# A fused decode block on one core: w2 in 27 and 29 rows, fewer VectorE instructions, the output projection in two column groups, gate and up in quadrants of 992 columns

## The chip, the cores and the metric

The kernel runs on one core of one Trainium2 chip. The metric is device time in microseconds (us), measured over several runs of one launch. Beside it stands one execution taken by the hardware profiler, which gives a page of views and a trace that can be asked for more. The engines are named as in the profile: PE is TensorE's matmul (PEld its weight load), DVE is VectorE, ACT is ScalarE, POOL is GpSimd, SP is SyncE, which issues nearly all DMAs here.

## What is computed

One decode step of a transformer block for 4 sequences: attention over the last 2048 positions of a cache, then a gated MLP, each behind a layer norm and with a residual. All data are bf16. Cut to what matters:

```python
B, Sq, D = 4, 1, 1024            # Hq, Hkv, Sk, Dh = 32, 4, 8192, 128; F = 3584; W = 2048

def A(x):                        # attention
    q = (x @ wq).reshape(B, Sq, Hq, Dh).transpose(0, 2, 1, 3)
    k = repeat(k_cache[:, :, Sk - W:, :], 8, axis=1)
    v = repeat(v_cache[:, :, Sk - W:, :], 8, axis=1)
    p = softmax(einsum("bhqd,bhkd->bhqk", q, k) * Dh ** -0.5)
    o = einsum("bhqk,bhkd->bhqd", p, v)
    return o.transpose(0, 2, 1, 3).reshape(B, Sq, Hq * Dh) @ wo

def M(x):                        # MLP
    return (silu(x @ w1) * (x @ w3)) @ w2

h = x + A(layernorm(x))
h2 = h + M(layernorm(h))
```

Each weight and each used row of the cache is read once: wq, wo 8 MB each, k and v 8 MB each, w1, w3 and w2 7 MB each. With 4 rows of activations there is little arithmetic for each byte.

## The kernel before

**The ring.** All large inputs go through `stream`, five slots of 32 KB a partition (4 MB). `ring` (line 107) lists what takes a slot, in order: k of sequences 0 and 1, k of 2 and 3, the first half of wq, two slots for the transposed keys kT (written by engines, no DMA), the second half of wq, v in two slots, wo in two, w1, w3 in two each, and w2 in two: 16 rows, then 8, 2 and 2 rows as three transfers (`W2B`, line 108). "Row" means one of the 28 rows of w2 that each of the 128 partitions holds. `fill` (line 119) issues on SP's queue, at line 133, all transfers for which a slot is free; `done` (line 140) is called where a part has been used and calls `fill`. The instructions of each engine stand in the order of the program; SP's issues wait in its queue for the semaphores of the engines that last used the slot. A transfer's landing is counted by 16 increments of a semaphore, one from each DMA engine.

**Stages, in the order of TensorE's instructions.**

- Constants (lines 147 to 190) are made on DVE and POOL; x is loaded on ACT's queue (line 149). `layernorm_T` (line 192) works on the transposed rows: squares, a matmul with ones for the sums, mean, variance, Sqrt on ACT (line 208), reciprocal, and the product into `n_T`.
- k: 256 transposes on TensorE (line 241), eight to a PSUM bank; the 32 banks are copied into kT by DVE and ACT in turn (lines 243, 245).
- q: wq in four column groups of 32 output rows each (line 259), copied to SBUF by DVE and ACT, half each (269, 270), transposed, and spread into `Qm` by four DVE copies (279).
- Attention: for each of the four sequences `scores` (four column groups, line 294), `row_max` (308 to 317), `softmax` (323 to 334, four Exp on ACT), `transpose_p` (a DVE transpose, 346), `output` (tot 355, o_ps 369, od 378 and om 386 on DVE). The loop at line 390 staggers them: TensorE starts the scores of one sequence while the one before is at its maximum.
- Output projection: on_ps (409), on_sb, oX, oP on DVE (417 to 422), then 128 matmuls of 256 columns, four column groups, `y_ps` (434); h1 adds x (444), then the second layer norm (LN2).
- MLP: `up_projection` (450) for w1 ("gate") and w3 ("up"), each in four column groups with 2 x 448 of the 896 columns of a group (458); Exp on ACT (472), add 1, reciprocal and product on DVE (473 to 476), hg (480), its transpose hg_T (482), and 112 matmuls with w2 into `y2_ps` (491, "y_ps" in the profile), residual (501) and two stores (503, 504).

The core of the ring:

```python
while len(taken) < len(ring):
    n = len(taken) - NSLOT
    if n >= 0 and not all((name, i) in used for name, i, _, _ in ring[n]):
        break
    parts = ring[len(taken)]
    slot = stream.tile([P, SLOT], BF16, tag="slot", name="s_" + parts[0][0])
```

Of the kernel before, what the change touches and what calls it, by code (L numbers as in the profile page):

```python
# [10 lines left out]
P = 128  # L11
# [12 lines left out]
def kernel(  # L24
# [30 lines left out]
    FC = F // P  # L55
# [5 lines left out]
    FQ = F // C  # L61
    FH = FQ // 2
    assert B == C and Hkv == C and B * Hq == P and Dh == P and REP * Hkv == R
    assert D == KC * P and F == FC * P and W == NK * P and NQ == Hq * Dh
# [14 lines left out]
    w2_v = B_w2.rearrange("(p fc) n -> p fc n", fc=FC)  # L79
# [21 lines left out]
    wo_ = pair([("wo", g, [1, T * D], wo_v[:, g : g + 1, :]) for g in range(Hkv)])  # L101
# [6 lines left out]
    W2B = [16, 8, 2, 2]  # L108
# [5 lines left out]
    ring += [w2_[:1], w2_[1:]]  # L114
# [4 lines left out]
    def fill():  # L119
# [7 lines that stand above are left out]
            o = 0  # L127
            for name, i, shape, src in parts:
                dst = slot[:, o : o + int(np.prod(shape))]
                o += int(np.prod(shape))  # L130
                view = dst.rearrange("p (a b) -> p a b", a=shape[0])
                if src is not None:
                    nc.sync.dma_start(out=dst if name in ("k", "v") else view, in_=src)  # L133
                views[(name, i)] = view
            taken.append(slot)
# [4 lines left out]
    def done(name, i):  # L140
# [7 lines left out]
    nc.vector.memset(x_nat[:], 0.0)  # L148
    nc.scalar.dma_start(out=x_nat[::S, :], in_=x_flat.rearrange("b (c n) -> c b n", c=C))
    fill()  # L150

    ident = const.tile([P, P], BF16)
    make_identity(nc, ident[:])
    ones_f = const.tile([P, P], FP32)
    nc.vector.memset(ones_f[:], 1.0)
    eps_t = const.tile([P, 1], FP32)
    nc.vector.memset(eps_t[:], eps)

    t32 = const.tile([P, R], FP32)
    nc.vector.tensor_reduce(  # L160
        out=t32[:], in_=ident[:].rearrange("p (q h) -> p h q", q=C), axis=AX.X, op=ALU.add
    )
    ident_f = const.tile([P, P], FP32)
    nc.gpsimd.tensor_copy(out=ident_f[:], in_=ident[:])
    same = const.tile([P, C, R], FP32)
    for q in range(C):
        nc.gpsimd.tensor_copy(out=same[:, q], in_=t32[:])
# [4 lines left out]
    nc.vector.tensor_scalar(  # L172
# [3 lines left out]
    nc.vector.tensor_reduce(  # L176
        out=jmask[:, :, 0], in_=ident[:].rearrange("p (j h) -> p j h", j=JM), axis=AX.X, op=ALU.add
    )
    nscale = const.tile([P, Hkv], FP32)
    nc.vector.memset(nscale[:], -qscale)  # L180
# [3 lines left out]
    for l in range(2):  # L184
        nc.gpsimd.tensor_copy(
# [6 lines left out]
    def layernorm_T(h_T, tag):  # L192

        both = act.tile([P, 2, KC, B], FP32, tag=tag + "_both")
        nc.vector.tensor_copy(out=both[:, 0], in_=h_T[:, :, ::S])
        nc.vector.tensor_tensor(out=both[:, 1], in0=both[:, 0], in1=both[:, 0], op=ALU.mult)  # L196
        sums_ps = ps.tile([P, 2, KC, B], FP32, tag="kt3")
        nc.tensor.matmul(sums_ps[:], lhsT=ones_f[:], rhs=both[:], start=True, stop=True)  # L198
        sums = act.tile([P, 2, B], FP32, tag=tag + "_sums")
        nc.vector.tensor_reduce(  # L200
            out=sums[:], in_=sums_ps[:].rearrange("p t k b -> p t b k"), axis=AX.X, op=ALU.add
        )
        mean = act.tile([P, 2, B], FP32, tag=tag + "_mean")
        nc.vector.tensor_single_scalar(out=mean[:], in_=sums[:], scalar=1.0 / D, op=ALU.mult)
        rstd = act.tile([P, 1, B], FP32, tag=tag + "_rstd")
        nc.vector.tensor_tensor(out=rstd[:, 0], in0=mean[:, 0], in1=mean[:, 0], op=ALU.mult)
# [7 lines left out]
        hc = act.tile([P, KC, B], FP32, tag=tag + "_hc")  # L214
# [14 lines left out]
    x_T = act.tile([P, KC, R], BF16)  # L229
# [5 lines left out]
    for b in range(B):  # L235
        k = get("k", b)
        kT = get("kT", b)
        for jb in range(JR // JB):
# [3 lines left out]
            if n_step % 2 == 0:  # L242
# [7 lines left out]
    q_ps = [ps.tile([P, REP // 2, Dh], FP32, tag=f"sc{hf}", name=f"q_ps{hf}") for hf in range(2)]  # L250
    HALF = REP // 2
    for i in range(KC // 4):
        w = get("wq", i)
        for kk in range(4):
            kc = 4 * i + kk
            for hf in range(2):
                for c in range(C):
                    o = (2 * c + hf) * HALF * Dh
                    nc.tensor.matmul(  # L259
                        q_ps[hf][R * c : R * c + R],  # L260
# [8 lines left out]
    nc.vector.tensor_copy(out=q_sb[:, :HALF], in_=q_ps[0][:])  # L269
    nc.scalar.copy(out=q_sb[:, HALF:], in_=q_ps[1][:])  # L270
# [7 lines left out]
    for b in range(B):  # L278
        nc.vector.tensor_copy(  # L279
            out=Qm[:, b].rearrange("p (g y) -> p g y", y=QW)[:, :, :REP],  # L280
            in_=qT_ps[:, :, :, S * b].rearrange("p r g -> p g r"),
        )


    sc_ps = [ps.tile([P, W // C], FP32, tag=f"sc{b}", name=f"sc_ps{b}") for b in range(B)]
    rs = act.tile([P, B, Hkv], FP32)
    om = act.tile([P, B, Dh], FP32)
    stage = {}

    def scores(b, gs):  # L290
        v = get("kT", b).rearrange("p j (q i g) -> p g q j i", q=C, g=Hkv)
        for g in gs:
            for q in range(C):
                nc.tensor.matmul(  # L294
                    sc_ps[b][R * q : R * q + R],
# [9 lines left out]
    def row_max(b):  # L305

        rmax = act.tile([P, 1], FP32, tag="rmax", bufs=2)
        nc.vector.reduce_max(out=rmax[:], in_=sc_ps[b][:], axis=AX.X)  # L308
        mx_ps = ps.tile([P, P], FP32, tag="kt3")
        nc.tensor.matmul(  # L310
            mx_ps[:1, :], lhsT=rmax[:], rhs=ident_f[:], start=True, stop=True
        )
        qmax = act.tile([1, C, R], FP32, tag="qmax", bufs=2)
        nc.vector.tensor_reduce(
            out=qmax[:, 0], in_=mx_ps[:1, :].rearrange("o (q h) -> o h q", q=C), axis=AX.X, op=ALU.max
        )
        nc.vector.tensor_copy(out=qmax[:, 1:], in_=qmax[:, 0:1].to_broadcast([1, C - 1, R]))
        stage[("qmax", b)] = qmax

    def softmax(b):  # L320

        nm_ps = ps.tile([P, Hkv], FP32, tag="kt3")
        nc.tensor.matmul(  # L323
            nm_ps[:],
            lhsT=stage.pop(("qmax", b))[:].rearrange("o q h -> o (q h)"),
            rhs=nscale[:1, :],
            start=True,
            stop=True,
        )
        bias = act.tile([P, Hkv], FP32, tag="bias", bufs=2)  # L330
        nc.vector.tensor_tensor(out=bias[:], in0=nm_ps[:], in1=negm[:], op=ALU.add)  # L331
        P4 = ktpool.tile([P, JR, L5, Hkv], BF16, tag="P4")
        for g in range(Hkv):
            nc.scalar.activation(  # L334
                out=P4[:, :, :, g],
                in_=sc_ps[b][:].rearrange("p (j i) -> p j i", i=L5),
                func=ACT.Exp,
                bias=bias[:, g : g + 1],
# [3 lines left out]
        stage[("P4", b)] = P4  # L342

# [9 lines left out]
    def output(b):  # L353
        tot_ps = ps.tile([P, Hkv], FP32, tag="kt3")
        nc.tensor.matmul(  # L355
            tot_ps[:],
            lhsT=same[:].rearrange("p q h -> p (q h)"),
            rhs=rs[:, b, :],
            start=True,
            stop=True,  # L360
        )
        rinv = act.tile([P, 1], FP32, tag="rinv", bufs=2)
        nc.vector.tensor_reduce(out=rinv[:], in_=tot_ps[:], axis=AX.X, op=ALU.add)
        nc.vector.reciprocal(out=rinv[:], in_=rinv[:])
# [3 lines left out]
        for i in range(JR // JM):  # L368
# [12 lines left out]
            scalar=rinv[:, 0:1],  # L381
# [4 lines left out]
        nc.vector.tensor_reduce(  # L386
            out=om[:, b], in_=od[:].rearrange("p j d -> p d j"), axis=AX.X, op=ALU.add
        )

    for b in range(B + 1):  # L390
        if b < B:
            scores(b, (0, 1))
        if b > 0:
            row_max(b - 1)
        if b < B:
            scores(b, (2, 3))
        if b > 0:
            softmax(b - 1)
        if b > 1:
            transpose_p(b - 2)  # L400
        if b > 2:
            output(b - 3)
    transpose_p(B - 1)
    output(B - 2)
    output(B - 1)
# [11 lines left out]
    nc.vector.tensor_copy(out=on_sb[:], in_=on_ps[:].rearrange("p l d -> p (l d)"))  # L417
    oX = act.tile([P, T, R], BF16)
# [3 lines left out]
    nc.vector.tensor_copy(  # L422
# [5 lines left out]
    y_ps = ps.tile([P, DQ], FP32, tag="kt0")  # L428
    for g in range(Hkv):
        w = get("wo", g)  # L430
        for t in range(T):
            for c in range(C):
                o = t * D + c * DQ
                nc.tensor.matmul(  # L434
                    y_ps[R * c : R * c + R, :],
                    lhsT=oP[:, g, t, :],
                    rhs=w[:, 0, o : o + DQ],
                    start=(g == 0 and t == 0),
                    stop=(g == Hkv - 1 and t == T - 1),
                    tile_position=(0, R * c),  # L440
                )
        done("wo", g)
    h1 = act.tile([P, DQ], FP32)
    nc.vector.tensor_tensor(out=h1[:], in0=y_ps[:], in1=x_nat[:], op=ALU.add)
    h_T = act.tile([P, KC, R], FP32)
    transpose_quads(h_T[:], h1[:], KC)
    hn_T = layernorm_T(h_T[:], "ln2")


    def up_projection(name, out_ps):  # L450
        for i in range(KC // 4):
            w = get(name, i)
            for kk in range(4):
                kc = 4 * i + kk
                for hf in range(2):
                    for c in range(C):
                        o = c * FQ + hf * FH
                        nc.tensor.matmul(  # L458
                            out_ps[hf][R * c : R * c + R],
# [8 lines left out]
    gu_ps = [ps.tile([P, FH], FP32, tag=f"sc{i}", name=f"gu_ps{i}") for i in range(4)]  # L468
    up_projection("w1", gu_ps[:2])
    eg = act.tile([P, 2, FH], FP32)  # L470
    for hf in range(2):
        nc.scalar.activation(out=eg[:, hf], in_=gu_ps[hf][:], func=ACT.Exp, scale=-1.0)
    nc.vector.tensor_scalar_add(out=eg[:], in0=eg[:], scalar1=1.0)
    nc.vector.reciprocal(out=eg[:], in_=eg[:])
    for hf in range(2):
        nc.vector.tensor_tensor(out=eg[:, hf], in0=gu_ps[hf][:], in1=eg[:, hf], op=ALU.mult)
    up_projection("w3", gu_ps[2:])
    hg = act.tile([P, 2, FH], BF16)
    for hf in range(2):
        nc.vector.tensor_tensor(out=hg[:, hf], in0=gu_ps[2 + hf][:], in1=eg[:, hf], op=ALU.mult)  # L480
    hg_T = act.tile([P, FC, R], BF16)
    transpose_quads(hg_T[:], hg[:].rearrange("p a f -> p (a f)"), FC)


    y2_ps = ps.tile([P, DQ], FP32, tag="kt1")
    fc = 0
    for i, n in enumerate(W2B):
        w = get("w2", i)
        for ff in range(n):
            for c in range(C):  # L490
                nc.tensor.matmul(  # L491
# [43 lines left out]
```

## Time and profile before

| | us |
|---|---|
| median of 3 runs | 140.03 (139.76, 140.03, 140.13) |
| the profiled execution's own time | 140.13 |
| its span in the profile | 138.3 |
| busy PE / PEld | 80.2 / 47.5 |
| busy DVE / ACT / POOL | 52.9 / 42.7 / 4.2 |
| DMA: 55.72 MB, mean | 403 GB/s |
| granted TensorE clock, mean | 0.781 |

The span is the time from the first instruction to the last; the device time has 1.8 us more around it. The page divides the span into 40 slices of some 3.5 us and shows the busy share of each engine in tenths, the granted clock of TensorE, and the share of time in which the 16 DMA engines moved data. The chain of waits is followed back from the last instruction: at each step to what released it. The timeline gives for each run of like instructions its start, its length, and, in brackets, the idle time of the engine before it and what ended that.

### The profile page before, as it was taken

How to read it: one execution, taken by the hardware profiler on the slowest of the kernel's cores; microseconds unless marked ns; L12 is line 12 of the kernel's file. 1: busy time of each engine (PE TensorE's matmuls, PEld its weight loads, DVE VectorE, ACT ScalarE, POOL GpSimd, SP SyncE). 2: the span in 40 equal slices, each digit the busy share in tenths (PEclk: the TensorE clock that was granted, in tenths of full speed). 3: DMA queues.
4: the chain of work that ended last, by engine and by line, in shares of the span. 5: the costliest groups of instructions: out<-in, count | busy, mean ns of one | idle time of the engine just before them, and what ended most of it. 6: DMA issues, size and time to landing. Idle time of an engine off the chain costs nothing.

```text
span 138.3 us, 2012 instructions
## 1 busy us (share of the span) xinstructions
PE 80.2 (58%) x866; PEld 47.5 (34%) x868; DVE 52.9 (38%) x97; ACT 42.7 (31%) x57; POOL 4.2 (3%) x18
## 2 busy tenths in 40 slices
PE   0029898921903889328918998659539901703780
PEld 0029887820301322014304434537324400202550
DVE  3036676520000235177087197540330298350001
ACT  3005988850000325998807900000040200000000
POOL 7400000000000000000000000000000000000000
PEclk9999999998555799975797799965865896555555
DMA  4999999999989999999999999999999999999930
GB/s 152 399 423 431 431 436 455 455 441 398 445 384 426 441 417 417 450 407 431 450 400 431 433 469 431 394 448 448 419 398 448 456 411 430 445 407 398 406 148 2
DMA packets 3217, 55.72 MB, mean 403 GB/s; under 512 B 360, under 2 KB 392, under 8 KB 648
## 3 DMA queue, kind: packets, MB, share of 16 engines
q1 hardware_dynamic: 3178, 55.58, 94.4%
q8 instruction: 7, 0.11, 0.3%
q10 hardware_dynamic: 30, 0.01, 0.0%
q14 instruction: 2, 0.02, 0.0%
HBM read 55.58 MB, written 0.01 MB: 402 GB/s over the span
## 4 chain that ended last, share of the span: by engine, by line
DMA 49%; PE 27%; DVE 13%; ACT 4%; SPq 3%; issue 2%; DVEq 0%
DMA s_wq<-in_A_wq_dram 29%; DMA s_w<-in_B_w_dram 20%; PE o_ps L369 10%; PE y_ps L434 5%; ACT P L334 4%; PE sc_ps L294 3%; DVE PT L346 3%; SPq L133 3%; PE gu_ps L458 2%; PE q_ps L259 2%; DVE om L386 2%; DVE od L378 2%; PE on_ps L409 1%; PE tot_ps L355 1%; PE nm_ps L323 1%
## 5 line engine op out<-in xcount | busy, mean ns | idle before, releaser
L334 ACT ACTIVATE P<-sc_ps,bias 128x512 bf16<-128x512 f32 x16 | 19.7, 1417 | 9.6 <-DVE bias L331 9.6
L241 PE MATMUL kt_ps<-ident,s_k 128*128 128x128 bf16 x256 | 17.3, 228 | 1.3 <-ACT s_kT L245 1.0
L369 PE MATMUL o_ps<-s_v,PT 128*128 128x512 bf16 x62 | 17.5, 439 | 0.3 <-issue 0.2
L241 PEld LDWEIGHTS <-s_k 128*128 128x128 bf16 x256 | 16.3, 103 | 2.3 <-issue 1.7
L245 ACT COPY s_kT<-kt_ps 128x1024 bf16<-128x1024 bf16 x16 | 15.7, 1012 | 2.5 <-PE kt_ps L241 2.5
L458 PE MATMUL gu_ps<-s_w,n_T 128*32 128x448 bf16 x128 | 10.7, 513 | 8.8 <-DMA s_w<-in_B_w_dram 6.8
L259 PE MATMUL q_ps<-s_wq,n_T 128*32 128x512 bf16 x64 | 7.0, 615 | 11.8 <-DMA s_wq<-in_A_wq_dram 11.8
L243 DVE COPY s_kT<-kt_ps 128x1024 bf16<-128x1024 bf16 x16 | 11.1, 693 | 5.8 <-PE kt_ps L241 5.8
L491 PE MATMUL y_ps<-s_w,hg_T 128*32 128x256 bf16 x112 | 6.6, 418 | 8.0 <-DMA s_w<-in_B_w_dram 8.0
L369 PEld LDWEIGHTS <-PT 128*128 128x128 bf16 x64 | 7.2, 117 | 9.2 <-issue 4.4
L346 DVE STREAM_TRANSPOSE PT<-P 128x2048 bf16<-128x2048 bf16 x4 | 9.2, 2303 | 2.7 <-ACT P L334 2.7
L208 ACT ACTIVATE rstd<-rstd,eps_t 128x4 f32<-128x4 f32 x2 | 0.6, 297 | 29.5 <-DVE rstd L207 29.5
L458 PEld LDWEIGHTS <-n_T 128*32 128x32 bf16 x128 | 4.7, 131 | 14.1 <-issue 11.6
L294 PE MATMUL sc_ps<-s_kT,Qm 128*32 128x512 bf16 x64 | 8.5, 603 | 0.4 <-DVE Qm L279 0.4
L491 PEld LDWEIGHTS <-hg_T 128*32 128x32 bf16 x112 | 4.9, 142 | 10.0 <-issue 5.9
L259 PEld LDWEIGHTS <-n_T 128*32 128x32 bf16 x64 | 2.7, 137 | 15.6 <-issue 15.5
L269 DVE CAST q_sb<-q_ps 128x512 bf16<-128x512 f32 x1 | 0.7, 692 | 18.3 <-PE q_ps L259 18.3
L198 PE MATMUL sums_ps<-both,ones_f 128*128 128x64 f32 x4 | 1.1, 373 | 11.2 <-DVE both L196 11.2
L434 PE MATMUL y_ps<-s_wo,oP 128*32 128x256 bf16 x128 | 6.5, 397 | 1.7 <-DVE oP L422 1.7
L378 DVE SCALAR_TENSOR_TENSOR od<-o_ps,rinv,jmask 128x512 f32<-128x512 f32 x4 | 3.0, 751 | 8.4 <-PE o_ps L369 8.3
L270 ACT CAST q_sb<-q_ps 128x512 bf16<-128x512 f32 x1 | 0.6, 585 | 17.8 <-PE q_ps L259 17.8
L310 PE MATMUL mx_ps<-ident_f,rmax 128*1 128x128 f32 x8 | 1.7, 302 | 7.4 <-DVE rmax L308 7.4
(68 smaller groups left out, 64.7 us busy)
## 6 DMA issues: line engine op xcount, KB each, us to landing
s_w<-in_B_w_dram SPq DMA_DIRECT2D x4, 3584.0 KB, 21.2
s_k<-in_A_k_cache_dram SPq DMA_DIRECT2D x4, 2048.0 KB, 16.1
s_wq<-in_A_wq_dram SPq DMA_DIRECT2D x2, 4096.0 KB, 35.3
s_v<-in_A_v_cache_dram SPq DMA_DIRECT2D x4, 2048.0 KB, 25.1
s_wo<-in_A_wo_dram SPq DMA_DIRECT2D x4, 2048.0 KB, 25.5
s_w<-in_B_w_dram SPq DMA_DIRECT2D x1, 4096.0 KB, 28.0
s_w<-in_B_w_dram SPq DMA_DIRECT2D x1, 2048.0 KB, 25.7
s_w<-in_B_w_dram SPq DMA_DIRECT2D x2, 512.0 KB, 27.0
```

The source lines that it names most:

```text
L241: nc.tensor.transpose(out=kt_ps[:, jj], in_=k[:, jb * JB + jj, :], identity=ident[:])
L243: nc.vector.tensor_copy(out=kT[:, jb * JB : (jb + 1) * JB], in_=kt_ps[:])
L245: nc.scalar.copy(out=kT[:, jb * JB : (jb + 1) * JB], in_=kt_ps[:])
L259: nc.tensor.matmul(q_ps[hf][R * c : R * c + R], lhsT=xn_T[:, kc, :], rhs=w[:, kk, o : o + HALF * Dh], start=(kc == 0), stop=(kc == KC - 1) ...
L294: nc.tensor.matmul(sc_ps[b][R * q : R * q + R], lhsT=Qm[:, b, g * R : (g + 1) * R], rhs=v[:, g, q], start=(g == 0), stop=(g == Hkv - 1), t ...
L334: nc.scalar.activation(out=P4[:, :, :, g], in_=sc_ps[b][:].rearrange("p (j i) -> p j i", i=L5), func=ACT.Exp, bias=bias[:, g : g + 1], sca ...
L346: nc.vector.transpose(out=PT[:].rearrange("p j h -> p (j h)"), in_=stage.pop(("P4", b))[:].rearrange("p j i g -> p (j i g)"),)
L369: nc.tensor.matmul(o_ps[:], lhsT=PT[:, i * JM : (i + 1) * JM, :].rearrange("p j h -> p (j h)"), rhs=v[:, i * JM : (i + 1) * JM, :], start= ...
L378: nc.vector.scalar_tensor_tensor(out=od[:], in0=o_ps[:], scalar=rinv[:, 0:1], in1=jmask[:].to_broadcast([P, JM, Dh]), op0=ALU.mult, op1=AL ...
L434: nc.tensor.matmul(y_ps[R * c : R * c + R, :], lhsT=oP[:, g, t, :], rhs=w[:, 0, o : o + DQ], start=(g == 0 and t == 0), stop=(g == Hkv - 1 ...
L458: nc.tensor.matmul(out_ps[hf][R * c : R * c + R], lhsT=hn_T[:, kc, :], rhs=w[:, kk, o : o + FH], start=(kc == 0), stop=(kc == KC - 1), til ...
L491: nc.tensor.matmul(y2_ps[R * c : R * c + R, :], lhsT=hg_T[:, fc, :], rhs=w[:, ff, c * DQ : (c + 1) * DQ], start=(fc == 0), stop=(fc == FC ...
```

## The change

- **w2.** FC is 27 instead of 28. The first 3456 rows of w2 are laid out as 27 rows for each partition; the last 128 rows (`w2x`) go to partitions 0 to 63 alone, two rows each, so that these hold 29 rows and the others 27. w2x is loaded by two transfers of 32 partitions (source shape 8 x 4 x 2048), at the head of the last slot, before 7, 2 and 2 rows. Its eight matmuls have 64 partitions of depth and stand after the first 16 rows.
- **Gate and up.** Each column group now starts at a multiple of 864 and takes 2 x 496 = 992 columns, so neighbours overlap by 128; the last group covers the columns that belong to w2x. PSUM is used as two tiles of two banks (`scA`, `scB`) for q, scores, gate and up.
- **VectorE.** Constants, squares, copies and the add of 1 move to ACT and POOL; only every fourth kT copy stays on DVE (ACT has the others); q_sb is one copy on ACT; Qm is one copy; the maximum is taken for two sequences at once; the mask is added by a matmul; the sums of two sequences come from four matmuls; od is added up by two POOL instructions. DVE has 37 rows of instructions in the program where it had 81.
- **Order.** The loop over sequences becomes a list written out: scores of 0 and 1, then one maximum for both, and so on in pairs.
- **Output projection.** wo comes in two transfers of 4 MB. y_ps has two column groups, each with 512 columns of a matmul (two blocks of 256 side by side); x is added by four matmuls with the identity; h1 is copied out by two DVE copies of 64 partitions.

```diff
-    FC = F // P
+    FC = F // P - 1
+    FM = FC * P
+    XP = P // 2
+    XR = 2
...
-    FQ = F // C
-    FH = FQ // 2
+    FQ = FM // C
+    FX = XP * XR
+    FH = (FQ + FX) // 2
...
-    w2_v = B_w2.rearrange("(p fc) n -> p fc n", fc=FC)
+    w2_v = B_w2[:FM].rearrange("(p fc) n -> p fc n", fc=FC)
+    w2x_v = B_w2[FM:].rearrange("(c i e y) n -> c e i (y n)", c=XP // R, i=4, e=8)
...
-    wo_ = pair([("wo", g, [1, T * D], wo_v[:, g : g + 1, :]) for g in range(Hkv)])
+    wo_ = [[("wo", i, [2, T * D], wo_v[:, 2 * i : 2 * i + 2, :])] for i in range(Hkv // 2)]
...
-    W2B = [16, 8, 2, 2]
+    W2B = [16, 7, 2, 2]
...
-    ring += [w2_[:1], w2_[1:]]
+    ring += [w2_[:1], [("w2x", 0, [XR, D], w2x_v)] + w2_[1:]]
...
+                if name == "w2x":
+                    for c in range(XP // R):
+                        nc.sync.dma_start(out=dst[R * c : R * c + R], in_=src[c])
...
-        nc.vector.tensor_copy(out=both[:, 0], in_=h_T[:, :, ::S])
-        nc.vector.tensor_tensor(out=both[:, 1], in0=both[:, 0], in1=both[:, 0], op=ALU.mult)
+        nc.scalar.copy(out=both[:, 0], in_=h_T[:, :, ::S])
+        nc.scalar.activation(out=both[:, 1], in_=h_T[:, :, ::S], func=ACT.Square)
...
-        nc.vector.tensor_tensor(out=rstd[:, 0], in0=mean[:, 0], in1=mean[:, 0], op=ALU.mult)
+        nc.scalar.activation(out=rstd[:, 0], in_=mean[:, 0], func=ACT.Square)
...
-            if n_step % 2 == 0:
+            if n_step % 4 == 0:
...
-    nc.vector.tensor_copy(out=q_sb[:, :HALF], in_=q_ps[0][:])
-    nc.scalar.copy(out=q_sb[:, HALF:], in_=q_ps[1][:])
+    nc.scalar.copy(out=q_sb[:], in_=q_ps[:].rearrange("p a r d -> p (a r) d"))
...
-        nc.vector.tensor_tensor(out=bias[:], in0=nm_ps[:], in1=negm[:], op=ALU.add)
+        bias = act.tile([P, 2, Hkv], FP32, tag="bias", bufs=2)
+        nc.scalar.copy(out=bias[:], in_=nm_ps[:])
...
-        nc.vector.tensor_reduce(
-            out=om[:, b], in_=od[:].rearrange("p j d -> p d j"), axis=AX.X, op=ALU.add
-        )
+        nc.gpsimd.tensor_tensor(out=o2[:], in0=od[:, :2], in1=od[:, 2:], op=ALU.add)
+        nc.gpsimd.tensor_tensor(out=om[:, b], in0=o2[:, 0], in1=o2[:, 1], op=ALU.add)
+
+    scores(0, (0, 1, 2, 3))
+    scores(1, (0, 1, 2, 3))
+    row_max(0)
+    scores(2, (0, 1))
+    bias_of(0)
+    softmax(0)
+    softmax(1)
+    scores(2, (2, 3))
+    scores(3, (0, 1, 2, 3))
+    row_max(1)
+    bias_of(1)
+    transpose_p(0)
+    transpose_p(1)
+    softmax(2)
+    softmax(3)
+    total(0)
+    output(0)
+    output(1)
+    transpose_p(2)
+    transpose_p(3)
+    total(1)
+    output(2)
+    output(3)
...
-    y_ps = ps.tile([P, DQ], FP32, tag="kt0")
+    y_ps = ps.tile([2 * R, 2, DQ], FP32, tag="kt0")
...
+            row = w[:, g % 2, t * D : (t + 1) * D].rearrange("p (k i n) -> p i k n", k=2, i=2)
+            for i in range(2):
                 nc.tensor.matmul(
-                    y_ps[R * c : R * c + R, :],
+                    y_ps[R * i : R * i + R],
                     lhsT=oP[:, g, t, :],
-                    rhs=w[:, 0, o : o + DQ],
+                    rhs=row[:, i],
...
-    nc.vector.tensor_tensor(out=h1[:], in0=y_ps[:], in1=x_nat[:], op=ALU.add)
+    for k in range(2):
+        nc.vector.tensor_copy(out=h1[XP * k : XP * k + XP, :], in_=y_ps[:, k])
...
-    nc.vector.tensor_scalar_add(out=eg[:], in0=eg[:], scalar1=1.0)
+    nc.scalar.activation(out=eg[:], in_=eg[:], func=ACT.Identity, bias=1.0)
...
+        if i == 0:
+            for y in range(XR):
+                down(hx_T[:, y, :], get("w2x", 0)[:XP, y], False, False)
```

## The prediction

> **What bounds the kernel now.** I read the busy slices first, then the chain of waits, then the timeline from 86 us, and last the issue and landing times of each weight transfer.
>
> ```profile
> PEclk9999999998555799975797799965865896555555
> DMA  4999999999989999999999999999999999999930
> ...
> q1 hardware_dynamic: 3178, 55.58, 94.4%
> q8 instruction: 7, 0.11, 0.3%
> ```
>
> The DMA row is at 9 from the second slice to the 38th: the engines never run dry. No compute engine is over 58%. The end of the chain of waits (start, length, what) says the same:
>
> ```profile
> 106.89 27.36 DMA s_w<-in_B_w_dram
> 134.26 0.04 issue
> 134.30 0.64 PE y_ps L491 x8
> 134.94 0.02 issue
> 134.97 0.42 DVE res L501
> ```
>
> The last transfer (two rows of w2) lands at 134.26; eight matmuls, one addition and the store follow. So the span is the DMA stream plus a fixed tail, and a change counts only if it (a) shortens the stream, (b) lets the queue run dry, or (c) makes the arithmetic later than the last landing.
>
> **The stream.** The trace records 16 landings for each transfer, one a DMA engine. For the first half of k they are at 7.80 to 8.01 (eight engines) and 8.11 to 8.36 (eight). For the last transfer seven are at 132.24 to 132.46, then 132.75, 133.06, 133.52, 134.04 and five at 134.14 to 134.26. So eight engines ("early") finish 1.5 to 2.0 us before most of the others ("late"), though all carry the same bytes. Packets of 16 KB take 0.61 us throughout, and those of 4 KB take 0.16 both when 16 engines run and when few are left: the limit is the single engine, not a shared one. The growing lag fits the fetches of q8, each some 1.06 us on one engine: after each, one more landing is late.
>
> The change gives every engine one row less in the third-last w2 transfer (8 partitions x 2 KB = 16 KB, 0.61 us) and sends 256 KB (w2x) in two transfers of eight outer steps. The load of x has four outer steps and its 16 packets ran on four engines; the store has two and ran on two. So w2x runs on eight engines, 32 KB each: 8 packets of 4 KB at 0.16 to 0.166, 1.3 us. Eight engines get 1.3 - 0.61 = 0.70 us more, eight get 0.61 less. Which eight the trace of before does not show; from both sides: on the early eight, the ends become 132.46 + 0.70 = 133.16 (the one at 132.75: 133.45) and 134.26 - 0.61 = 133.65, a **gain of 0.61**; on late ones 134.26 + 0.70 = 134.96, a **loss of 0.70**. I take the gain: the four engines of x are among the early eight (without x's packets, four of these end k at 7.41 to 7.44; the four with them at 7.59 to 7.77).
>
> The Trainium skill, "DMA: Bandwidth & Descriptors", section "Why a DMA increments its semaphore by 16 and not by 1", says that such a DMA uses the lowest-numbered engines, which would be the right eight; no run here numbers them. Its "Rules for kernel authors" speak against small and eight-engine transfers, with about 2 us of fixed cost for each; here the last two 512 KB transfers land 1.24 and 1.29 us apart, back to back, so that cost isn't seen in a filled queue. By the rule, two transfers could add up to 4 us.
>
> **Does the queue stay filled?** SP issues a transfer when its slot is free. Issue time, and when the queue would then have been empty: v01 28.5, 43.8; v23 37.8, 53.6; wo01 47.3, 63.5; wo23 52.8, 73.3; w1 62.8, 83.1 and 79.2, 91.6; w3 87.3, 100.1 and 95.9, 108.6; w2 98.8, 117.1; the rest 106.0, 126.8. The smallest reserve is 12.4 us. What the edits do to these times:
>
> - kT copies: ACT has 24 of 32 instead of 16. "1.95 x2" on the timeline is 0.975 each: 23.4 us from about 12.4, to 35.8; before, 28.6. v01 is issued near 35: 8.8 us of reserve. q then waits for wq's landing (43.86) as before.
> - One q_sb copy on ACT: about 1.0 (0.58 for half), against 0.69 and 0.58 side by side; one Qm copy for four. Scores start at 49.3 (48.8).
> - Two batches at once: 32 score matmuls at 0.1075 (3.5), a maximum over 1024 (about 1.2; 0.69 for 512), mx, qmax and nm some 1.9. The order of instructions also puts the table load of Exp (1.28) behind the bias copy, so the first exp starts at 57.4 instead of 53.3. But the 16 exps then run almost without the 5 us gap at 68.4 to 73.6 (DVE had od, om and rmax ahead of the bias): 8 x 1.19, about 1 us of hand-over, 8 x 1.19, to 77.6 (78.5).
> - total, od, PT: output(1) ends near 77.8 (79.2), PT2 and PT3 by 83.2, output(3) at 88.2 (87.3).
> - om on POOL: no row of POOL adds two tensors. Bounds 0.58 (two casts of 0.29) and 1.9 (two memsets of 0.95); I take 1.1 by the 128x128 cast, DVE had 1.04.
> - The constants on POOL and ACT end before x lands (8.36): nothing; without that cover they would delay LN1 alone, which has until 34.1.
>
> So w1's second half is issued at about 78, w3's at 88 and 99.7, w2 at 102.4, the rest at 111: reserves of 9 us or more. All this costs **nothing**. One wo transfer for two changes no bytes.
>
> **Is the arithmetic late?** This is the dangerous part. The timeline from 86 us (start, length, engine, line, operation):
>
> ```profile
> 92.28 6.50 PE L434 MATMUL y_ps<-s_wo,oP 128*32 128x256 bf16 x128 [1.73 <-DVE oP L422]
> ...
> 110.28 5.75 DVE L474 RECIPROCAL eg<-eg 128x896 f32<-128x896 f32 x1
> ...
> 121.21 1.70 DVE L225 STREAM_TRANSPOSE hg_T<-hg 128x896 bf16<-128x896 bf16 x1
> ...
> 126.88 3.61 PE L491 MATMUL y_ps<-s_w,hg_T 128*32 128x256 bf16 x64 [6.53 <-DMA s_w<-in_B_w_dram]
> 131.77 2.33 PE L491 MATMUL y_ps<-s_w,hg_T 128*32 128x256 bf16 x40 [1.28 <-DMA s_w<-in_B_w_dram]
> ```
>
> Before, hg_T is ready at 122.9, 4 us before w2 lands. After:
>
> 1. y starts at 88.2 + 0.75 + 1.1 + 1.4 (on_ps) + 0.4 + 0.65 + 0.4 = 93.0 (92.3).
> 2. y: 64 matmuls of 512 columns in two column groups. At the granted clock of 0.50 four groups of 256 took 0.203, that is four streams side by side; 512 columns at this clock take 0.427 (o_ps from 64 us). Two groups side by side: 32 x 0.427 = 13.7 if the clock stays at 0.50; 32 x 0.215 = 6.9 at 1.00. The view of windows (stretch, then sum and each engine's busy time; the last three columns are granted clock, DMA share and GB/s) shows 0.50 from 92.2 and 0.99 from 98.1, and the same rise inside gate:
>
> ```profile
> 92.20:98.10 5.90, 5.82 (x112) 4.30 (x116) 0.03 (x1) 0.00 (x0) 0.00 (x0) 0.50 1.03 442
> 98.10:99.00 0.90, 0.69 (x24) 0.38 (x16) 0.16 (x1) 0.00 (x0) 0.00 (x0) 0.99 1.04 446
> 102.80:108.30 5.50, 5.48 (x60) 2.42 (x64) 0.00 (x0) 0.57 (x1) 0.00 (x0) 0.50 1.02 438
> 108.70:110.40 1.70, 1.65 (x36) 0.89 (x32) 0.75 (x2) 0.89 (x2) 0.00 (x0) 1.00 0.94 405
> ```
>
> After a pause the clock was 0.50 for 3.1 (q at 43.9) to 5.8 us of matmuls, then 1.00. With 4.6: 10.8 pairs, then 21.2 at 0.215, together **9.2**; y ends at 102.2 (98.8). Whether half-filled columns raise the clock no row shows; both ends stay in the range.
>
> The skill's "TensorEngine Tiling (Array Packing)", section "Theoretical Speedup", gives up to four-fold for 32 columns, so two groups would take twice as long: 13 us. The trace agrees at one clock; the rise of the clock is what saves it.
>
> 3. LN2: two h1 copies (0.75 for 0.44), and the table load of Sqrt, which in before ran at 78.6 in ACT's idle time, now stands behind Square: 1.28 less the 0.2 of the subtraction beside it. Moving both, Square and the mean to ACT and PE nets nothing. 4.0 becomes 5.5: gate starts at 107.75 (102.8).
> 4. gate: 64 matmuls of 496 at 0.103 (0.0932 for 448) while the clock is low, then half: 5.6, to 113.4.
> 5. Exp and Identity on ACT over 992: about 1.05 each (0.98 for 896); reciprocal 5.75 x 992/896 = 6.4; product 1.3: 123.2. up is done by 120.5 (w3 lands at 117.1).
> 6. hg 1.3, hg_T 1.7: **126.1**. w2 lands at 126.8.
>
> From 126.88, w2 costs 116 matmuls at 0.0564 (3.61/64) = 6.5 us, and the last eight cannot start before 133.65. So hg_T may be as late as 127.7: a margin of 1.6 us, where it was 4.8. hx_T (two small transposes) and the w2x matmuls (8, 0.45) lie in the wait before 131.1, when the seven rows land.
>
> **Sum.** Stream -0.61, queue 0, arithmetic 0, tail 0. The profiled execution took 140.13 (span 138.3, 1.8 around it): 139.5. It is the highest of three; from the median 140.03 I forecast **139.4**.
>
> **Rivals.**
>
> - *TensorE becomes the last.* If y stays at 0.50, y takes 4.45 more, hg_T comes at 130.55, 116 matmuls end at 137.1 instead of 134.94: +2.1, **142.1**. It decides from 1.6 us of added delay on, then 1 us for 1 us. For it: the low clock and the 6.4 us reciprocal on the path. Against it: every stretch of dense matmuls over 6 us here ends at 1.00. Chance 0.17. A mild form (POOL's upper bound, a long low clock) eats the gain: 139.6 to 140.7, 0.08.
> - *w2x goes to late engines:* +0.70, **140.7**. Against it: x's four engines. 0.08.
> - *The balance does nothing,* since a fetch hits one late engine twice and that one sets the end: **140.0**. 0.07. With 116 rows fewer for TensorE there should rather be one fetch less.
> - Forecast, 139.1 to 139.8: 0.60.
>
> A measurement of this kernel tells about 0.3% (0.42 us) from no change. Faster: most of the forecast, some of the mild form, 0.57; same 0.15; slower 0.28 (0.17 + 0.08 + 0.03). The range goes from 139.0 to the end where y stays slow, 142.2; the likeliest case's own is 139.1 to 139.8.
>
> **What would show it.** The last transfer's landings: early eight near 133.1, late near 133.65. DMA at 9 throughout; SP's issues as listed. y near 9 us, with the clock rising inside it; the table load between Square and Sqrt; hg_T done before 127. I am wrong if the last step of the chain is hg_T or y2 without a DMA ahead of it, or if one group of landings is at 135.

## The result, and the profile after

After takes **140.66 us** (median of 7 runs, 140.45 to 140.91 but for one of 141.4), before 140.03 (7 runs, 139.76 to 140.16): ratio 1.0051, 95% interval 1.0038 to 1.0064. The change makes the kernel slower by 0.63 us, where 0.6 us of gain was forecast.

| profiled execution | before | after |
|---|---|---|
| own time / span | 140.13 / 138.3 | 140.77 / 138.7 |
| last landing of the last transfer | 134.26 | 134.67 |
| y starts / gate starts | 92.3 / 102.8 | 98.4 / 111.0 |
| last matmul ends | 134.94 | 135.42 |

Start with the difference of time and span in every run: before 1.83 (mean of 23 runs), after **2.04** (7 runs). Of the 0.63 us, 0.2 lie outside the span, and no view of the span can show them. The mean span rose by 0.5, from 138.2 to 138.7.

The busy slices and queues of after (q8 and q14 are queues of kind "instruction": they bring the engines' code, and the experiments below tell whose):

```profile
PEclk9999999999965558996555995999999559995559
DMA  4999999999989999999999999999999999989920
...
q8 instruction: 6, 0.10, 0.3%
q14 instruction: 1, 0.01, 0.0%
```

The DMA row is at 9 up to the slice in which the stream ends, so the queue never ran dry. Code was fetched once less on q8 than before. The chain of waits at the end (start, length, what) no longer ends in a DMA:

```profile
111.01 5.25 PE gate L502 x48
...
118.38 6.37 DVE eg L520
...
124.83 1.20 DVE eg L521
...
126.13 1.20 DVE hg L523
127.36 1.66 DVE hg_T L234
129.02 0.04 issue
129.06 6.36 PE y_ps L542 x89
135.44 0.42 DVE res L561
```

TensorE starts w2 at 129.06 and has no pause until 135.42. But the chain hides a second bound as near: the last two landings are at 134.63 and 134.67, and before, landing and last matmul were 0.68 apart. 134.67 + 0.68 = 135.35: without any delay in the arithmetic, after would have ended 0.07 us earlier. (In experiments 1 and 11 below the distance is 0.48 and 0.47, so up to 0.28 earlier is possible.) In this execution the later landing alone is 0.41 us, of the 0.48 by which the last matmul is late.

The trace's landings of one transfer are a clock for each DMA engine. They carry no engine's number, but the lags stay the same to a few hundredths from one transfer to the next, so that they can be followed. For the 16 rows of w2 (the last large transfer), worked out as lag behind the first of the 16 landings:

```
before  0.00 0.10 0.14 0.17 0.20 0.22 0.23 0.53 0.85 1.32 | 1.86 1.96 1.97 1.98 2.00 2.04
after   0.00 0.01 0.10 0.10 0.13 0.17 0.18 0.18 0.20 0.37 0.88 | 1.62 1.64 1.65 1.68 1.79
```

Six engines are far behind before, five after. Ahead of this transfer q8 fetched code six times before (20.5 to 112.9 us) and five times after (23.6 to 114.8). So there are not eight early and eight late engines, as the prediction took it, but as many late ones as q8 fetches. The lags between the two groups, 0.85 and 1.32 before and 0.88 after, go with q14, whose fetches are of 8 KB. Before has two of them in its stream, at 69.9 and 77.7 us:

```profile
q14 instruction: 2, 0.02, 0.0%
```

After has one in its stream, at 36.9 us, and a second one behind the end of its span.

The eight landings of w2x itself tell who its engines are: 125.56 to 125.73 (five), **126.44, 127.20, 127.25**. Three of w2x's eight engines were behind already: one by 0.88 us (q14's), two by 1.64 and 1.69 (q8's).

### The profile page after: what moved, and what is told of

The parts are those of the page before. It is cut to its first block, busy times and chain, and to the rows that moved or that the text cites. A ratio compares the mean times of both kernels' runs of the same rounds, so it can differ in the third digit from the quotient of the medians.

```text
span 138.7 us, 1900 instructions
## 1 busy us (share of the span) xinstructions
PE 82.4 (59%) x814; PEld 48.9 (35%) x816; DVE 37.1 (27%) x46; ACT 57.0 (41%) x93; POOL 8.8 (6%) x28
## 4 chain that ended last, share of the span: by engine, by line
PE 37%; DMA 29%; DVE 14%; ACT 13%; SPq 2%; issue 2%; POOL 1%; POOLq 0%; DVEq 0%; ACTq 0%
DMA s_wq<-in_A_wq_dram 29%; PE o_ps L389 13%; ACT P L352 7%; PE y_ps L474 5%; DVE eg L520 5%; PE y_ps L542 5%; PE gate L502 4%; PE sc_psscA L302 3%; PE q_ps L268 3%; SPq L143 2%; DVE PT L377 2%; PE tot_ps L366 1%; DVE hg_T L234 1%; DVE od L398 1%; PE on_ps L436 1%
## 5 line engine op out<-in xcount | busy, mean ns | idle before, releaser
L254 ACT COPY s_kT<-kt_ps 128x1024 bf16<-128x1024 bf16 x24 | 22.4, 1076 | 1.4 <-PE kt_ps L250 1.4
L250 PE MATMUL kt_ps<-ident,s_k 128*128 128x128 bf16 x256 | 20.3, 245 | 4.1 <-ACT s_kT L254 3.3
L352 ACT ACTIVATE P<-sc_psscB,bias 128x512 bf16<-128x512 f32 x8 | 9.7, 1422 | 0.0
L352 ACT ACTIVATE P<-sc_psscA,bias 128x512 bf16<-128x512 f32 x8 | 9.7, 1425 | 0.0
L252 DVE COPY s_kT<-kt_ps 128x1024 bf16<-128x1024 bf16 x8 | 5.5, 694 | 14.4 <-PE kt_ps L250 14.4
L542 PE MATMUL y_ps<-s_w,hg_T 128*32 128x256 bf16 x64 | 3.6, 419 | 9.5 <-DVE hg_T L234 9.5
L520 DVE RECIPROCAL eg<-eg 128x992 f32<-128x992 f32 x1 | 6.4, 6355 | 7.4 <-ACT eg L519 7.4
L407 POOL TENSOR_TENSOR o<-od 128x256 f32<-128x256 f32 x4 | 2.9, 724 | 82.9 <-DVE od L398 82.9
L474 PE MATMUL y_ps<-s_wo,oP 128*32 128x512 bf16 x64 | 7.1, 379 | 1.6 <-ACT oP L449 1.6
L502 PE MATMUL gate<-s_w,n_T 128*32 128x496 bf16 x64 | 5.2, 501 | 2.9 <-DVE n_T L227 2.9
```

The costliest lines, as they stand in the source:

```text
L250: nc.tensor.transpose(out=kt_ps[:, jj], in_=k[:, jb * JB + jj, :], identity=ident[:])
L252: nc.vector.tensor_copy(out=kT[:, jb * JB : (jb + 1) * JB], in_=kt_ps[:])
L254: nc.scalar.copy(out=kT[:, jb * JB : (jb + 1) * JB], in_=kt_ps[:])
L352: nc.scalar.activation(out=P4[:, :, :, g], in_=sc_ps[b // 2][:, b % 2].rearrange("p (j i) -> p j i", i=L5), func=ACT.Exp, bias=bias[:, b % ...
L474: nc.tensor.matmul(y_ps[R * i : R * i + R], lhsT=oP[:, g, t, :], rhs=row[:, i], start=False, stop=(g == Hkv - 1 and t == T - 1), tile_posi ...
L502: nc.tensor.matmul(out_ps[R * c : R * c + R, hf, :FH], lhsT=hn_T[:, kc, :], rhs=w[:, kk, o : o + FH], start=(kc == 0), stop=(kc == KC - 1) ...
```

## The experiments

Two theories to begin with. **S (stream):** each fetch puts one engine behind for good; w2x adds 0.70 us to eight engines, some of them late; the last of them sets the end. **A (arithmetic):** w2x balances as forecast, and only the late start of w2's matmuls costs.

**1. w2x alone.** The kernel before with the w2 part of the change (columns of gate and up follow from it):

```diff
-    w2_v = B_w2.rearrange("(p fc) n -> p fc n", fc=FC)
+    w2_v = B_w2[:FM].rearrange("(p fc) n -> p fc n", fc=FC)
+    w2x_v = B_w2[FM:].rearrange("(c i e y) n -> c e i (y n)", c=XP // R, i=4, e=8)
-    W2B = [16, 8, 2, 2]
+    W2B = [16, 7, 2, 2]
```

> The kernel before with the w2 part alone: 27 and 29 rows, w2x, gate and up in 992 columns; all other instructions as before. Theory S (stream): the engines that are late are those that an instruction fetch has hit, and some of them are among the eight that carry w2x, so their +0.70 us sets the end; expects the last landing near 134.7 and a time of 140.3 to 140.7. Theory A (arithmetic): the changed kernel is slower only because w2's matmuls start late; here hg_T keeps 4 us of margin, so the balance pays: last landing near 133.65, time near 139.4.

Measured 140.66 (140.31 to 140.77), ratio 1.0040 (1.0026 to 1.0054), with 1.81 around the span. The profile is of the fastest run, 140.31; its chain of waits:

```profile
111.48 23.02 DMA s_w2x<-in_B_w_dram
134.50 0.04 issue
134.54 0.44 PE y_ps L505 x8
134.98 0.02 issue
135.00 0.42 DVE res L524
```

The arithmetic is that of before, the end is a DMA's, and it is late: S. The last landing is 134.50, that of before 134.26. Two of w2x's eight landings are behind, 0.78 and 1.18 us after the first of them (the next is at 0.25).

Here the lags tell more than S said. Those of the 16 rows of w2 are 0.00 to 0.55 (eight engines), 0.87, 1.28, and 1.68 to 1.93 (six, for six q8 fetches). Take 0.09, 0.10, 0.11, 0.12, 0.20, 0.34, 0.87 and 1.28 as w2x's eight and add 1.27 us to each (eight packets of 0.16), and the sixteen lags of the next transfer come out within 0.03. So w2x's engines are eight of the ten that q8 did not hit. The six late ones did gain: their last landing is 133.86, 0.40 earlier than before. The end at 134.50 belongs to the engine that was 1.28 behind and got w2x on top, and that lag is one of the two that go with q14, not q8. What this trace does not show is the whole loss: its run took 140.31, 0.35 less than the median.

**2. w2x on 16 engines.** After with `i=2, e=16` in place of `i=4, e=8` (and in hx_T): 0.04 us more (0.70 less 0.61, halved) for every engine, so no imbalance.

> The changed kernel with the w2x transfers laid out with 16 outer steps instead of 8, so that they run on 16 engines and every engine has the bytes it had before. Both theories expect the landings to end as before (about 134.2). Theory S expects a gain of at most 0.1 us against the changed kernel, since TensorE would still end at 135.4: 140.5 to 140.7. Theory A expects no change: 140.7, with hg_T at 129 again.

Measured 142.60, ratio 1.0182 (1.0168 to 1.0196): both missed. With 16 engines writing to 32 partitions the packets themselves became slow. Between 124 and 129 us, those of 4 KB took 0.16 to 0.48 us (median 0.24; 0.16 else), their neighbours of 14 KB 0.71 to 1.39 (median 0.95; 0.54 else), and of 32 KB 1.40 to 2.44 (median 2.36; 1.22 else); the last landing was 136.59. So this run could not be the control it was meant to be. That the shared partitions are the reason is not shown apart from other effects of the layout.

**3. After, another order:** the arithmetic made 4 us earlier.

```diff
     output(0)
-    output(1)
     transpose_p(2)
+    output(1)
     transpose_p(3)
```

> The changed kernel with the DVE transposes PT of the second pair moved up: PT of sequence 2 ahead of od of sequence 1, PT of sequence 3 behind it. TensorE should not pause 2.4 us at 82 us, its clock should not fall there, and all that follows should come some 3 us earlier: hg_T at 126 instead of 129. Theory A expects the balance to show then: last landing near 133.65, 139.4. Theory S expects the last landing to stay near 134.7, and 140.4 to 140.6.

Measured 140.49 (140.33 to 140.60, but for one run of 193.04, which the ratio leaves out), ratio 1.0029 (1.0018 to 1.0041). y started at 94.46 instead of 98.40, and the chain of waits ended in the DMA:

```profile
113.02 21.57 DMA s_w2x<-in_B_w_dram
134.60 0.04 issue
134.64 0.64 PE y_ps L542 x7
135.28 0.02 issue
135.30 0.42 DVE res L561
```

Four us earlier hardly help (140.66 to 140.49, with ratio intervals that overlap), because the stream is right behind: A falls as the main cause, though some 0.2 us of the loss may be its.

**4. The same order, w2x on 16 engines.**

> Both edits: PT moved up and w2x on 16 engines. Arithmetic about 3 us earlier and no shift of bytes. Theory S expects the time of before: 139.9 to 140.1, clearly less than with PT moved up alone. Theory A expects the time of before too, but that is more than with PT moved up alone (139.4). The sign of the difference between the two decides.

Measured 142.30, ratio 1.0161 (1.0147 to 1.0175), last landing 136.43: the slow packets again.

**5. Few instructions.** S rests on the fetches, so they were taken away: TensorE has 225 instructions where before has 1665.

```diff
-            for jj in range(JB):
-                nc.tensor.transpose(out=kt_ps[:, jj], in_=k[:, jb * JB + jj, :], identity=ident[:])
+            nc.tensor.matmul(
+                kt_f[:, 0], lhsT=ident[:], rhs=k[:, jb * JB : jb * JB + JB // 2, :], start=True, stop=True
+            )
...
-        for i in range(JR // JM):
+        for i in (JR // JM - 1,):
...
-            for kk in range(4):
+            for kk in (3,) if i == 1 else ():
```

> The kernel before with 225 instructions on TensorE instead of 1665: most matmuls are left out (k is not transposed but multiplied by the identity in blocks, and of q, scores, o, y, gate, up and w2 only one part in four to sixteen is done), so the output means nothing; every byte is still loaded by the same transfers in the same order. Theory S (each 16 KB fetch of code on q8 puts one DMA engine some 1.6 us behind for good, and the last such engine sets the end): the six q8 fetches ahead of the end are gone, and with them the six landings of the last transfer at 134.04 to 134.26; the last lands near 133.0 (two fetches of q14 remain, 0.7 each), time 138.8 (138.2 to 139.2). Theory F (as the prediction took it: eight of the engines are late by themselves, fetches only add to it): a late group remains near 134.2, time 139.9 to 140.1.

Measured 139.69 (139.53 to 139.90), ratio 0.9977 (0.9968 to 0.9986): between the two forecasts. The page's queues tell why:

```profile
q8 instruction: 1, 0.02, 0.0%
q14 instruction: 2, 0.02, 0.0%
```

One q8 fetch was left, and one engine more than 1.4 us behind. That one landed last, at 133.97; the next at 133.48. Theory F (a fixed late group) has nothing to show for it, and S learns that **one** late engine costs nearly as much as six: its landing is 0.29 us ahead of before's. (Four matmuls follow it here instead of eight, 0.40 us for 0.64, so not all of the 0.31 us in time need be the stream's.)

**6. Few instructions, with w2x.**

> The same kernel with few TensorE instructions, and w2 in 27 and 29 rows as in the first experiment. Theory S: with no engine late, w2x only unbalances: eight engines end at 132.4 + 0.7 = 133.1 (one of them hit by a q14 fetch: up to 133.8), the others at 131.7 to 132.4; time 138.9 to 139.5, that is 0 to 0.7 above the kernel without w2x. Theory F: w2x gives to the early eight, 0.61 is gained against the kernel without w2x.

Measured 139.97 (139.85 to 140.55), 0.28 above experiment 5; the last landing is 134.27, 0.30 later. The three late engines now lagged 1.00, 1.05 and 1.69; two of them are among w2x's eight (landings of w2x: six at 125.76 to 125.81, then 126.76 and 126.81). F's gain of 0.61 is not there. As in experiment 1, the two of w2x's engines that were behind are q14's (two 8 KB fetches, lags 1.00 and 1.05), and they set the end; the q8 one (1.69) carries no w2x and lands its last part at 133.63, 0.34 earlier than in experiment 5.

**7. After, the order of experiment 3, without w2x** (28 rows, 896 columns, every other edit as in after).

> The kernel after with the order of the third experiment and with w2 as before (28 rows, gate and up 896 columns a group, no w2x): every other edit stays. Theory S: five late engines, last landing near 134.2, TensorE waits for it, time 139.9 to 140.1, ratio 0.999 to 1.001; all of the loss of the third experiment was w2x's. Rival (the other edits cost something of their own, through SP's issues or the end): 140.3 to 140.5 again.

Measured 140.43 (140.28 to 140.56), ratio 1.0030 (1.0020 to 1.0040). This went against S as it stood: w2x was gone, and the time had not come back. The chain of waits has a DMA landing at 134.27 and the span is that of before, 138.2. All of the 0.4 us is outside the span: 2.22 around it (8 runs). Behind its end the trace has one entry that the trace of before has not: an 8 KB fetch on q14, at 140.25. After has it at 139.85, experiment 3 at 139.70.

**8. More instructions.** Before with 128 matmuls of one column ahead of q.

> The kernel before with 128 more matmuls of one column (256 instructions) ahead of q, where TensorE waits for wq; their result is not used. Theory S: one more q8 fetch ahead of the end (seven), seven late landings of the last transfer instead of six, time the same within 0.2 (140.0 to 140.2) unless the fetch falls on an engine already late, then the last landing is near 135.8 and the time 141.6. Theory F: the landings stay as before.

Measured 140.18 (one run). Seven q8 fetches ahead of the 16 rows of w2, and seven landings 1.54 to 1.91 behind the first. Over twelve kernels (all but the two with 16 engines) the number of engines over 1.4 us late equals the number of q8 fetches ahead: 1, 1, 5 (six kernels), 6 (three) and 7. In the same twelve, the number of engines 0.65 to 1.32 behind equals the number of q14's 8 KB fetches in the stream, one or two; all others are at most 0.55 behind. (The bounds were drawn after seeing the lags.)

**9. VectorE padded.** What the fetch behind the end belongs to. Experiment 7 with 30 instructions more on VectorE:

```diff
+    spare = const.tile([P, 1], FP32)
+    for _ in range(30):
+        nc.vector.memset(spare[:], 0.0)
     ident = const.tile([P, P], BF16)
```

> The kernel of the seventh experiment with 30 tiny memsets on VectorE at the start, where VectorE waits for x. The seventh had the span of before (138.2) but 2.2 us around it instead of 1.8, and its trace, like that of after, shows an 8 KB fetch of code (q14) 1.2 to 2.0 us behind the end of the span, which no kernel with VectorE's old number of instructions has. Theory T: this fetch is VectorE's; with few instructions its next block of code is needed only at the very end of the program, where nothing hides it. With 30 more, the fetch moves into the stream (an 8 KB fetch near 80 to 120 us, one engine 0.7 later), none stands behind the span, the time around it is 1.8, the time 140.0 (139.9 to 140.2; 140.6 if the engine hit is a late one). Rival T2: the fetch is ScalarE's (twice the instructions of before): nothing changes, 140.4. Rival T3: the fetch moves but the time around the span stays 2.2: 140.4.

Measured **140.01** (139.70 to 140.06), ratio 0.9992 (0.9983 to 1.0000), 1.79 around the span. The page's queue and the chain:

```profile
q14 instruction: 2, 0.02, 0.0%
```

```profile
109.34 24.89 DMA s_w<-in_B_w_dram
134.23 0.04 issue
134.28 0.65 PE y_ps L536 x7
```

The second q14 fetch has moved to 83.9 us, into the stream, and nothing is fetched behind the span. Theory T holds, in place, span and time: 30 instructions more make the kernel 0.4 us faster.

**10. ScalarE relieved.** Experiment 7 with 14 constants on GpSimd instead of ScalarE.

> The kernel of the seventh experiment with 14 small constant instructions moved from ScalarE to GpSimd. Theory T (the fetch behind the span is VectorE's): still there, 2.2 around the span, 140.4. Rival T2 (it is ScalarE's): gone or at another place, 1.8 around the span, 140.0.

Measured 140.56, ratio 1.0033 (1.0020 to 1.0046), 2.29 around the span; the fetch behind it is still there (139.95). What moved is the other q14 fetch, from 36.8 to 73.5 us: that one is ScalarE's. T2 falls.

**11. After, VectorE padded.**

> The kernel after with the 30 tiny memsets on VectorE at the start. Theory T: no fetch behind the span, 1.8 around it instead of 2.04, span as in after (138.7): 140.45 (140.3 to 140.6). Rivals T2 and T3: 140.66 as after.

Measured 140.44 (140.35 to 140.57), ratio 1.0030 (1.0019 to 1.0041), 1.79 around the span: 0.22 less than after, as T has it. The last landing is 134.83, against 134.23 in experiment 9, and the chain of waits ends in that landing with 0.43 of matmuls behind it: this is after's own order, and the arithmetic is not last in it. With the fetch put right, what stays is w2x (experiment 9 differs in the order too, which by experiment 3 is worth some 0.2).

**12. A try at beating both.** Before with `W2B = [16, 8, 2, 1, 1]`.

> A try at beating both: the kernel before with w2 as 16, 8, 2, 1 and 1 rows, so that behind the last landing four matmuls stand instead of eight. The bytes of each engine are the same, so the last landing should stay at 134.2 to 134.3; four matmuls took 0.40 in the kernel with few instructions where eight took 0.64 in before: time 139.75 (139.6 to 139.9). Rival: packets of 2 KB instead of 4 KB cost each engine some 0.1 to 0.3 more (4 KB take 0.160, that is 40 ns a KB against 38 for 16 KB): 139.9 to 140.1.

Measured 139.88 (139.70 to 140.09), ratio 0.9994 (0.9985 to 1.0002): no difference that this can tell. In the profile the last four matmuls take 0.29 where eight took 0.64, at the same last landing (134.20):

```profile
134.24 0.29 PE L491 MATMUL y_ps<-s_w,hg_T 128*32 128x256 bf16 x4 [0.34 <-DMA s_w<-in_B_w_dram]
```

No version that does the whole computation beat before by more than the measurement can tell.

## Why the prediction was wrong, point by point

**The failed step: "I take the gain: the four engines of x are among the early eight."** The two groups that it chose between do not exist as groups. As many engines are late as q8's (and, by less, q14's) fetches were made, and the early landings of k, at 8 us, say nothing of it: the first fetch comes at 20.5. The prediction had seen the clue ("after each, one more landing is late") and used it only for a rival. It counted the landings at 133.06 and 133.52, those that go with q14, to the late ones and took w2x's eight to be the other eight. In experiments 1 and 6 the eight held the two q14 engines and none of q8's; in after one of q14's and two of q8's. The landing moved by +0.41 instead of -0.61.

The packets were costed rightly: an engine with w2x moved 1.27 us behind one without (1.31 forecast), and in experiment 1 the engines that q8 had hit did end 0.40 earlier. The loss that the prediction priced (+0.70) was right in kind for after: late engines of w2x's eight got later and set the end. Its size was too large, since the late ones among the eight lagged 1.6 to 1.7 and not the 2.0 of the last one before. For w2x to gain, none of its engines may be far behind; even with one q8 fetch in all (experiment 6) two of the eight were 1.0 behind.

**"A fetch hits one late engine twice" (rival).** Not seen in the twelve kernels above: each q8 fetch made another engine late. The part on TensorE's fewer matmuls was right, five fetches for six, and worth nothing: experiment 5 shows that one late engine sets the end nearly as late as six (133.97 for 134.26).

**Queue: costs nothing.** Right. Without w2x, with the other order and VectorE padded, all other edits together make 140.01.

**Arithmetic: 0, with 1.6 us of margin.** The steps were the right ones, but the margin was used up, and so the term was not 0 but 0.1 to 0.3. hg_T was done at 129.02, not 126.1; the limit was 127.7. Nearly all of it is step 1: y at 98.4, not 93.0 (its terms add up to 92.9); y itself gave 2 us back. In the timeline of after (start, length, engine, line, operation, idle time ahead):

```profile
81.87 4.50 DVE L377 STREAM_TRANSPOSE PT<-P 128x2048 bf16<-128x2048 bf16 x2
...
84.23 8.51 PE L389 MATMUL o_ps<-s_v,PT 128*128 128x512 bf16 x31 [2.35 <-DVE PT L377]
...
98.40 2.98 PE L474 MATMUL y_ps<-s_wo,oP 128*32 128x512 bf16 x25 [1.63 <-ACT oP L449]
```

The transpose of sequence 2 stands in VectorE's order behind od of sequence 1, which waits for TensorE; so TensorE waits for it in turn, 2.35 us, and then runs at a granted clock of 0.50 (84.2 to 86.4 us; before had 1.00 from 78 to 91). I had PT2 and PT3 done by 83.2. Experiment 3 takes that wait away, and gate starts 4.1 us earlier. The tot matmuls took 1.9 us ahead of output(0), oP on ACT 0.76 (0.4 expected).

**y: 9.2 (6.9 to 13.7).** 7.08 measured: the clock was 1.00 throughout. The reason is not shown: TensorE stood idle ahead of y for 1.63 us in after and for 1.73 in before, where the clock then was 0.50 up to 98.1. Two groups of 512 columns took 7.1 at full clock where four of 256 had taken 6.5, mostly at half. The factor of two that the prediction drew from the Trainium skill ("TensorEngine Tiling (Array Packing)", "Theoretical Speedup") comes out at one clock: 24 matmuls of 256 columns in four groups took 0.69 at 0.99 (before), 64 of 512 in two groups 7.08 at 1.00 (after), 1.9 times as long for a column.

**LN2 5.5, gate 5.6, Exp and Identity 1.05 each, reciprocal 6.4, product 1.3, hg_T 1.7.** Measured 5.5, 5.25, 1.01 and 1.04, 6.37, 1.20, 1.66. The table load stood behind Square, as foreseen.

**Tail and "1.8 around": 0.** Wrong by 0.2, and not looked at: the change was costed inside the span only. Fewer instructions on VectorE moved its last fetch of code to where nothing hides it.

**The cost of two more transfers.** The last two transfers of after land 1.25 to 1.28 us apart, the two of w2x some 0.6, back to back; so the 2 us for each that the prediction cites are not seen in a filled queue. The section that it names has no such figure; the Trainium skill's page "DMA: Bandwidth & Descriptors" gives it under "Anatomy of one DMA — SWDGE (gpsimd) path", as a fit for DMAs issued from GpSimd, and these are issued by SP. Whether w2x has the lowest-numbered engines no trace here shows.

**The sum as it is.** In span, 0.5: the late landing from w2x (0.4 in the profiled execution) and TensorE's late start (0.1 to 0.3 beyond it, by the tails above and by experiment 3). Outside, 0.2: the fetch. By experiments: w2x alone +0.65; padding after takes 0.22 off; all edits but w2x, mended, 140.01. The parts do not add exactly, as w2x cost 0.28 us (experiment 6) to 0.65 (experiment 1), and which of its engines the fetches hit differs from kernel to kernel. What decides on which engine a fetch falls stays open.

## What to carry to other kernels

Where the stream bounds a kernel, read the landings of a late transfer one engine at a time and set them beside the code fetches: the end belongs to the engine that is furthest behind, and a transfer that uses only some engines may gain only if none of those is late. Cost a change outside the span too: an instruction more or less can move a fetch into the stream or out behind the end. And when a chain ends in an engine, work out how far behind it the next bound is, before making that engine faster.

## What the hardware showed that was not expected

- A fetch of 16 KB on q8 takes 0.9 to 1.1 us on one engine, and one engine more is then 1.4 to 2.0 us behind the first of the sixteen for the rest of the stream. One of 8 KB on q14 takes 0.3 to 0.4 us and goes with a lag of 0.65 to 1.32.
- An 8 KB fetch that falls behind the end of the span goes with 0.2 us of time (after) to 0.5 (experiment 10), though it takes 0.3 to 0.5 itself.
- 16 engines writing 4 KB packets into the same 32 partitions (experiments 2 and 4) went with packets of up to 0.48 us instead of 0.16, and their neighbours of 14 KB took 0.67 to 1.39 instead of 0.54; with eight engines they stayed at 0.16 to 0.17.
